# A rarely taken branch moved from between two stages to the end of the kernel

## The chip, the cores and the metric

One core of one Trainium2 chip runs the whole kernel. The metric is the device time of one execution in microseconds (us); lower is better. A core has five engines with instruction queues of their own: TensorE (PE in the profile, with its weight loads as PEld), VectorE (DVE), ScalarE (ACT), GpSimd (POOL) and SyncE (SP, which here only issues DMAs). Engines wait for one another through semaphores; a trailing q in the profile (DVEq, SPq) marks what an engine's sequencer does itself: loads of registers, branches, semaphore instructions.

## The reference, cut to what matters

Three blocks follow each other: a bucketed attention, a mixture of 8 experts in which every token goes to one expert, and a dense two-layer block.

```python
attn_out = _attn_ref(q, k, v, proj)                 # (2, 8, 768, 64)
x = attn_out.transpose(0, 2, 1, 3).reshape(1536, 512)

# experts: each token goes to the expert with the largest logit
expert_idx = np.argmax(x @ w_gate, axis=1)
for e in range(8):
    mask = expert_idx == e
    h = np.maximum(x[mask] @ w1[e], 0.0)            # 512 -> 1024
    out[mask] = gate_w[mask, None] * (h @ w2[e])    # 1024 -> 512

# last stage
h = x @ w_in                                        # 512 -> 2048
g = np.where(h > 0.0, h, np.exp(np.minimum(h, 0.0)) - 1.0)
return g @ w_out                                    # 2048 -> 512
```

## The kernel before, in words

The order of instructions on every engine is the order of the Python code (`tc.manual_schedule()`); the framework adds the semaphores, from which tile regions an instruction reads and writes.

**Attention** (`attention`) leaves the rows of x in DRAM (`g.xd`) and the gate logits in SBUF. **Routing** (`routing`) sorts the tokens by expert: `g.idx` holds for each sorted place the row it came from, `g.offi` the first place of each expert.

**Experts** (`moe`). Twelve gathers (`gather`, L762, an indirect DMA issued by POOL) fetch 128 sorted rows each. `gate` (L772, a DVE `tensor_scalar` on 128x512 fp32 in SBUF, in place) multiplies them by their gate weight, and `turn` transposes them on PE (L783) into `g.xhl`, two fp16 parts, with one ACT and one DVE instruction (L785, L789). From tile 2 on these are interleaved with the first expert's matmuls: in slot i of `rest(i)` the gates of slot i+1 are issued first, then the turns of slot i, then `more()` issues one further gather. The experts are 16 products in the order of `SEQ`; each reads a window of NW = 224 columns at an offset known only at run time. `expert_up` (L851 to L857) makes the hidden layer, `expert_down` (L869 to L876) writes columns of `g.yh` (ACT, L875) and `g.yl` (DVE, L876), one of four planes d at a time, each accumulated by 24 matmuls. Weights come in by SP (L572) into six or seven staging buffers and are split into two fp16 parts by a `Feeder` on ACT (L613) and DVE (L587 to L589, L609); during the last experts it splits `w_in` into `g.wih` and `g.wil`.

**The branch.** An expert with more than 224 tokens needs further windows. `overflow_table` lists them in `g.ovi`, with their count first. After the last expert every engine loads the count into a register (L1031) and branches on it (L1032). If it is over 0, a loop loads that expert's weights again and runs up and down for one window per round. Where a path skips such a block, each engine brings the semaphores to the values that the other path would have left.

**Last stage** (`moe2`). `stage1(b)` makes for 512 tokens 16 groups of 12 matmuls from `g.wih`, `g.wil`, `g.yh` and `g.yl` (L1087 to L1089) with an ACT, DVE and POOL chain behind each group (L1092 to L1108); `stage2` multiplies by `w_out` (L1116 to L1118) and stores by an indirect DMA from POOL that puts the rows back in order (L1122, L1123). `w_out` is loaded by SP at the start of `moe2` and split while the stage runs. PSUM is a ring of 8 banks in both stages. `body` calls `attention`, `moe` and `moe2`; L1241 is where the program ends, with drains and a barrier of all engines.

Of the kernel before, what the change touches and what calls it, by code (L numbers as in the profile page):

```python
# [9 lines left out]
F16 = mybir.dt.float16  # L10
F32 = mybir.dt.float32
I32 = mybir.dt.int32
# [3 lines left out]
PSUM = bass.MemoryType.PSUM  # L16
# [6 lines left out]
NT = B * S  # L23
DM = H * D
E = 8
# [30 lines left out]
STG = 6  # L56
# [578 lines left out]
WX = NT + NW  # L635
NOV = NT // NW
JOV = -(-NT // NW) - 1
XS, W1S, W2S, YS = 2.0 ** 6, 2.0 ** 6, 2.0 ** 7, 2.0 ** 13
# [122 lines left out]
def gather(nc, g, j, x):  # L761
    nc.gpsimd.indirect_dma_start(out=x, out_offset=None, in_=g.xd, in_offset=bass.IndirectOffsetOnAxis(ap=g.idx[:, j:j + 1], axis=0))  # L762
    g.xg[j] = x


def gate(nc, g, j, act=False):

    x, w = g.xg[j], g.gws[:, j:j + 1]
    if act:
        nc.scalar.activation(x, x, AF.Copy, scale=w)  # L770
    else:
        nc.vector.tensor_scalar(x, x, w, None, op0=ALU.mult)  # L772


def turn(tc, g, ps, js):

    nc = tc.nc
    PT = []
    for j in js:
        x = g.xg.pop(j)  # L780
        pt = ps.tile([128, 4, 128], F32, tag="mp", bufs=8, name="pt")
        for c in range(4):
            nc.tensor.transpose(pt[:, c], x[:, c * 128:(c + 1) * 128], g.id32)  # L783
        cols = slice(j * 128, (j + 1) * 128)
        nc.scalar.activation(g.xh[:, :, cols], pt, AF.Copy)  # L785
        PT.append((j, pt))
    for j, pt in PT:
        cols = slice(j * 128, (j + 1) * 128)
        nc.vector.tensor_sub(g.xl[:, :, cols], pt, g.xh[:, :, cols])  # L789


def overflow_table(tc, g, pool):

    nc = tc.nc
    sh = [1, E, JOV]
    off, n = g.oc[:, 0], g.oc[:, 1]
    jw = g.jw.unsqueeze(1).to_broadcast(sh)
    t = pool.tile([1, 4, E, JOV], F32, name="ovt")
    fl, st, pl, ex = (t[:, i] for i in range(4))
    nc.vector.tensor_tensor(fl, n.unsqueeze(2).to_broadcast(sh), jw, op=ALU.is_gt)  # L800
    nc.vector.tensor_tensor(st, off.unsqueeze(2).to_broadcast(sh), jw, op=ALU.add)
    sc = pool.tile([1, 4, 16], F32, name="osc")
    nc.vector.memset(sc, 0.0)
    en = sc[:, 3, 0:8]
    nc.vector.tensor_tensor(en, off, n, op=ALU.add)
    yield
    nc.vector.tensor_scalar(en, en, float(-NW), None, op0=ALU.add)
    nc.vector.tensor_tensor(st, st, en.unsqueeze(2).to_broadcast(sh), op=ALU.min)
    nc.vector.tensor_reduce(sc[:, 0, 8:16], fl, axis=AX.X, op=ALU.add)
    nc.vector.tensor_add(sc[:, 1, 8:16], sc[:, 0, 8:16], sc[:, 0, 7:15])  # L810
    yield
    nc.vector.tensor_add(sc[:, 2, 8:16], sc[:, 1, 8:16], sc[:, 1, 6:14])
    nc.vector.tensor_add(sc[:, 3, 8:16], sc[:, 2, 8:16], sc[:, 2, 4:12])

    nc.vector.tensor_tensor(en, sc[:, 3, 8:16], sc[:, 0, 8:16], op=ALU.subtract)
    nc.vector.tensor_tensor(pl, g.iota12[0:1, 1:1 + JOV].unsqueeze(1).to_broadcast(sh), en.unsqueeze(2).to_broadcast(sh), op=ALU.add)
    yield
    nc.vector.tensor_mul(pl, pl, fl)
    nc.vector.tensor_scalar(ex, g.iota8[0:1].unsqueeze(2).to_broadcast(sh), 8.0, None, op0=ALU.add)
    g.ovi = pool.tile([1, 1 + 2 * NOV], I32, name="ovi")  # L820
    ov = pool.tile([1, 1 + 2 * NOV], F32, name="ov")
    nc.vector.tensor_copy(ov[:, 0:1], sc[:, 3, 15:16])
    sw = [1, NOV, E * JOV]
    hw = pool.tile([1, 2, NOV, E * JOV], F32, name="hw")
    wb = g.iota12[0:1, 1:1 + NOV].unsqueeze(2).to_broadcast(sw)
    nc.vector.tensor_tensor(hw[:, 0], pl.rearrange("o e j -> o (e j)").unsqueeze(1).to_broadcast(sw), wb, op=ALU.is_equal)
    yield
    for x, o in ((ex, 1), (st, 1 + NOV)):
        nc.vector.tensor_mul(hw[:, 1], hw[:, 0], x.rearrange("o e j -> o (e j)").unsqueeze(1).to_broadcast(sw))
        nc.vector.tensor_reduce(ov[:, o:o + NOV], hw[:, 1], axis=AX.X, op=ALU.add)  # L830
    nc.vector.tensor_copy(g.ovi, ov)


def window(nc, g, pool, off):

    xw = pool.tile([128, 2, 4, NW], F16, tag="xw", bufs=2, name="xw")
    nc.vector.tensor_copy(xw[:, 0], g.xh[:, :, ds(off, NW)])
    nc.vector.tensor_copy(xw[:, 1], g.xl[:, :, ds(off, NW)])
    return xw[:, 0], xw[:, 1]


def expert_up(nc, pool, ps, wh, wl, xh, xl, step):

    hh = pool.tile([128, 8, NW], F16, tag="hh", bufs=2, name="hh")
    hl = pool.tile([128, 8, NW], F16, tag="hl", bufs=2, name="hl")
    for f in range(8):
        p = ps.tile([128, NW], F32, tag="mp", bufs=8, name="hp")
        fs = slice(f * 128, (f + 1) * 128)
        for kk in range(4):
            w = slice(kk * 1024 + f * 128, kk * 1024 + (f + 1) * 128)  # L850
            nc.tensor.matmul(p, lhsT=wh[:, w], rhs=xh[:, kk], start=(kk == 0), stop=False)  # L851
            nc.tensor.matmul(p, lhsT=wl[:, w], rhs=xh[:, kk], start=False, stop=False)
        for kk in range(4):
            w = slice(kk * 1024 + f * 128, kk * 1024 + (f + 1) * 128)
            nc.tensor.matmul(p, lhsT=wh[:, w], rhs=xl[:, kk], start=False, stop=(kk == 3))
        nc.scalar.activation(hh[:, f], p, AF.Relu)
        nc.vector.scalar_tensor_tensor(hl[:, f], p, 0.0, hh[:, f], op0=ALU.max, op1=ALU.subtract)  # L857
        step(f)
    return hh, hl


def expert_down(nc, g, ps, wh, wl, hh, hl, offs, step, pre=lambda d: None):

    s = YS / (XS * W1S * W2S)
    for d in range(4):
        p = ps.tile([128, NW], F32, tag="mp", bufs=8, name="yp")
        for kk in range(8):
            w = slice(kk * 512 + d * 128, kk * 512 + (d + 1) * 128)
            nc.tensor.matmul(p, lhsT=wh[:, w], rhs=hh[:, kk], start=(kk == 0), stop=False)  # L869
            nc.tensor.matmul(p, lhsT=wl[:, w], rhs=hh[:, kk], start=False, stop=False)  # L870
        for kk in range(8):
            w = slice(kk * 512 + d * 128, kk * 512 + (d + 1) * 128)
            nc.tensor.matmul(p, lhsT=wh[:, w], rhs=hl[:, kk], start=False, stop=(kk == 7))
        pre(d)
        nc.scalar.activation(g.yh[:, d, ds(offs[0], NW)], p, AF.Copy, scale=s)  # L875
        nc.vector.scalar_tensor_tensor(  # L876
            g.yl[:, d, ds(offs[1], NW)], p, s, g.yh[:, d, ds(offs[1], NW)], op0=ALU.mult, op1=ALU.subtract)
        step(d)


def w_items(we, x, scale, n=None):

    m = 1024 // we.shape[1]
    v = we.rearrange("(k p) f -> p k f", p=128)
    return [((v[:, c * m:(c + 1) * m], "p (k f) -> p k f", dict(k=m)), False,
             lambda c=c: tuple(a[:, 1024 * c:1024 * c + 1024] for a in x()), scale, n)
            for c in range(4)]


def moe(tc, es, g, w_gate, w1, w2, fd):  # L890
    nc = tc.nc
# [18 lines left out]
    for n in range(3, 2 * E):  # L910
        e, which = SEQ[n]
# [5 lines left out]
    for e in range(1, E):  # L917
        m = min(8, len(items) - a)
        last = e == E - 1
        n = m + XN[e] + (WO7 + 2 if last else 0)  # L920
# [10 lines left out]
    def more():  # L931
        nonlocal gathered
        if gathered < 12:

            k = gathered % 8
            gather(nc, g, gathered, g.wih.rearrange("p k f -> p (k f)")[:, k * 1024:(k + 1) * 1024].bitcast(F32))
            gathered += 1

    offs = [], []

# [87 lines left out]
    assert not fd.left()  # L1028


    n = nc.values_load(g.ovi[0:1, 0:1], min_val=0, max_val=NOV)  # L1031
    with tc.If(n > 0):  # L1032
        with tc.For_i(0, n, 1) as i:
            e = nc.values_load(g.ovi[0:1, ds(i + 1, 1)], min_val=0, max_val=E - 1)
            st = nc.values_load(g.ovi[0:1, ds(i + 1 + NOV, 1)], min_val=0, max_val=NT)
            fo = Feeder(nc, g, STG)
            fo.eager, fo.mode32 = True, ("ad", "ad")
            fo.add(w_items(w1[ds(e, 1)].rearrange("o k f -> (o k) f"), lambda: W[0], W1S))
            fo.add(w_items(w2[ds(e, 1)].rearrange("o k f -> (o k) f"), lambda: W[2], W2S))
            fo.load()  # L1040
            while fo.left():
                fo.step()
            xw = window(nc, g, pool, st)
            hh, hl = expert_up(nc, pool, ps, *W[0], *xw, lambda f: None)
            expert_down(nc, g, ps, *W[2], hh, hl, [st, st], lambda d: None)


def w_out_items(w_out, parts, cs, phase, g):
# [169 lines left out]
                moe2(tc, es3, g, w_out, out, fd)  # L1218


_INS = ["q", "k", "v", "proj", "moe_w_gate", "moe_w1", "moe_w2", "moe2_w_in", "moe2_w_out"]
_OUTS = [((NT, DM), "float32")]

# [22 lines left out]
```

## Time and profile before

| | us |
|---|---|
| three timed runs, median | 680.91 |
| lowest and highest of them | 678.58, 682.52 |
| the profiled execution, own time | 680.53 |
| its span, first to last instruction | 678.6 |

| engine | busy us | share of the span |
|---|---|---|
| PE matmul | 637.6 | 94% |
| DVE | 487.1 | 72% |
| ACT | 363.7 | 54% |
| POOL | 268.8 | 40% |

The profiled execution is inside the spread of the timed ones; 1.9 us of its time lie outside its span. The page lists 64 loads of expert weights of 512 KB each: 16 matrices in 4 pieces. With these inputs the loop of the branch thus runs no round, for a round would load 8 pieces more. Of 40 slices of the span, POOL is idle in nine in a row, from about 270 to 425 us. Attention takes the span up to about 250 us, routing and experts up to 420 us, the last stage the rest.

### The profile page before, as it was taken

What the parts mean: (1) busy time and instruction counts of PE and PEld (TensorE: products, weight loads), DVE (VectorE), ACT (ScalarE), POOL (GpSimd) and SP (SyncE); (2) the same over time, 40 slices, a digit from 0 to 9 for tenths busy, and PEclk for the clock granted to TensorE, in tenths of its full rate; (3) what the DMA queues carried; (4) which work ended last, traced back from release to release, by engine and by line L of the source; (5) the groups of instructions that cost most, each with busy time, mean ns of one, the idle gap of its engine ahead of it and who ended that gap; (6) DMA issues with size and microseconds to landing.
All of it is one profiled execution on the core that took longest, in us unless ns stands there. A gap on an engine that the chain in (4) does not pass through costs nothing. (4 is left out here: it accounts for less than half of the span.)

```text
span 678.6 us, 12321 instructions
## 1 busy us (share of the span) xinstructions
PE 637.6 (94%) x4615; PEld 422.9 (62%) x4615; DVE 487.1 (72%) x980; ACT 363.7 (54%) x664; POOL 268.8 (40%) x329
## 2 busy tenths in 40 slices
PE   5899988999999875999999998999999999999996
PEld 3456666666666644999999997444444444444442
DVE  6778989888976446899999998578788919900000
ACT  4566676667667633667666572575754237600000
POOL 4868778686854017000000000486866024411101
PEclk9989999999999998999999999999999999999999
DMA  5797999999683016477888791511111110000000
GB/s 176 159 169 174 195 268 236 203 229 197 140 142 93 13 41 204 158 272 261 292 277 307 264 286 43 202 34 55 39 37 68 52 47 16 1 15 32 23 24 31
DMA packets 124544, 92.87 MB, mean 137 GB/s; under 512 B 94273, under 2 KB 106561, under 8 KB 124481
## 3 DMA queue, kind: packets, MB, share of 16 engines
q1 hardware_dynamic: 122528, 85.76, 47.3%
q0 software_dynamic: 1952, 6.30, 2.7%
q8 instruction: 37, 0.61, 0.4%
q14 instruction: 27, 0.21, 0.1%
HBM read 62.94 MB, written 6.29 MB: 102 GB/s over the span
## 5 line engine op out<-in xcount | busy, mean ns | idle before, releaser
L1100 POOL TENSOR_SCALAR gh<-m 128x512 f16<-128x512 f32 x48 | 39.0, 812 | 198.0 <-DVE m L1099 198.0
L337 ACT ACTIVATE A<-sp,nm 128x768 f32<-128x768 f32 x96 | 95.0, 991 | 35.0 <-DVE nm L330 28.8
L319 DVE TENSOR_REDUCE nm<-sp 128x1 f32<-128x768 f32 x96 | 91.0, 948 | 25.4 <-PE sp L315 24.0
L378 ACT ACTIVATE AT<-ptA 128x512 f32<-128x512 f32 (+1 forms) x102 | 59.0, 580 | 39.5 <-PE ptA L376 32.7
L1087 PE MATMUL p<-yh,wih 128*128 128x512 f16 x192 | 73.5, 383 | 2.7 <-DVEq L1032 2.7
L388 PE MATMUL ot<-AT,vraw 128*64 128x384 f32 x192 | 74.2, 507 | 1.8 <-ACT AT L378 1.8
L1088 PE MATMUL p<-yl,wih 128*128 128x512 f16 x192 | 73.5, 383 | 0.0
L1089 PE MATMUL p<-yh,wil 128*128 128x512 f16 x192 | 73.3, 382 | 0.0
L376 PE MATMUL ptA<-id,A 128*128 128x128 f32 x396 | 61.8, 280 | 10.7 <-ACT AT L378 9.1
L314 PE MATMUL sp<-KA,QA 128*128 128x384 f16 x192 | 63.6, 331 | 3.3 <-ACT A L337 3.0
L376 PEld LDWEIGHTS ptA<-id,A 128*128 128x128 f32 x396 | 46.4, 141 | 31.4 <-ACT AT L378 26.0
L1098 DVE SCALAR_TENSOR_TENSOR m<-ex,th 128x512 f32<-128x512 f32 x48 | 37.1, 773 | 38.9 <-ACT th L1096 32.0
L315 PE MATMUL sp<-KB,QB 76*128 76x384 f16 x192 | 63.1, 329 | 0.7 <-DMA KB<-krb 0.7
L1122 ACT ACTIVATE o<-p 128x512 f32<-128x512 f32 x12 | 7.2, 597 | 86.7 <-PE p L1118 81.2
L1123 POOL DMA_INDIRECT out_dram<-o,idx x12 | 11.9, 990 | 104.8 <-ACT o L1122 102.3
L1094 ACT ACTIVATE ex<-r,lngs 128x512 f32<-128x512 f32 x48 | 34.7, 722 | 34.2 <-DVE m L1098 33.6
L347 POOL TENSOR_TENSOR hl<-A,hl 128x768 f16<-128x768 f32 x30 | 49.6, 1652 | 2.5
L1102 POOL TENSOR_TENSOR gl<-m,gh 128x512 f16<-128x512 f32 x32 | 46.2, 1444 | 2.7
L393 PE MATMUL ot<-ATD,VH 128*64 128x256 f16 x270 | 46.0, 280 | 0.0
L397 PE MATMUL ot<-AT,vraw 128*64 128x128 f32 (+1 forms) x192 | 40.0, 291 | 0.0
L358 POOL TENSOR_SCALAR hl<-A 128x768 f16<-128x768 f32 x30 | 25.0, 835 | 35.9 <-ACT A L337 35.9
L1116 PE MATMUL p<-wbh,gh 128*128 128x512 f16 x96 | 36.4, 379 | 0.1
(251 smaller groups left out, 1634.0 us busy)
## 6 DMA issues: line engine op xcount, KB each, us to landing
stg<-in_moe_w_dram SPq DMA_DIRECT2D x64, 512.0 KB, 4.6
stg<-in_moe_w_in_dram SPq DMA_DIRECT2D x16, 512.0 KB, 4.8
stg<-in_moe_w_out_dram SPq DMA_DIRECT2D x16, 512.0 KB, 3.2
vraw<-in_v_dram SPq DMA_DIRECT2D x8, 384.0 KB, 3.8
xd<-xr SPq DMA_DIRECT2D x16, 192.0 KB, 2.4
qraw<-in_q_dram SPq DMA_DIRECT2D x7, 384.0 KB, 3.9
kraw<-in_k_dram SPq DMA_DIRECT2D x7, 384.0 KB, 4.2
ATD<-hl SPq DMA_TRANSPOSE x30, 3.6
```

What stands on the lines that cost most here:

```text
L314: nc.tensor.matmul(sp[:, j, 0:384], lhsT=QA[P, h][:, c * 128:(c + 1) * 128], rhs=KA[P, h][:, kk], start=True, stop=False)
L315: nc.tensor.matmul(sp[:, j, 0:384], lhsT=QB[P, h][0:76, c * 128:(c + 1) * 128], rhs=KB[P, h][0:76, kk], start=False, stop=True)
L319: nc.vector.tensor_reduce(nm[:, 0:1], sp[:, :, 0:384], axis=AX.XY, op=ALU.max, negate=True)
L337: nc.scalar.activation(a, sp[:, :, 0:384], AF.Exp, bias=nm[:, 2:3], scale=nm[:, 1:2], accum_out=SUM[u][:, r:r + 1])
L347: LATE.append((lambda: nc.gpsimd.tensor_tensor(hl[:, 1], a, hl[:, 0], op=ALU.subtract), u, r, hl, a))
L376: nc.tensor.transpose(pt[:, cols], src[:, kt * 128:(kt + 1) * 128], g.id32)
L378: nc.scalar.activation(at[:, 0:n], pt[:, 0:n], AF.Copy)
L388: nc.tensor.matmul(ot[64:128], lhsT=vt[P][:, 1, kt, :], rhs=at, start=(kt == 0), stop=(kt == 5))
L1087: nc.tensor.matmul(p, lhsT=g.wih[:, kk, fs], rhs=g.yh[:, kk, cols], start=(kk == 0), stop=False)
L1088: nc.tensor.matmul(p, lhsT=g.wih[:, kk, fs], rhs=g.yl[:, kk, cols], start=False, stop=False)
L1089: nc.tensor.matmul(p, lhsT=g.wil[:, kk, fs], rhs=g.yh[:, kk, cols], start=False, stop=(kk == 3))
L1102: nc.gpsimd.tensor_tensor(gl[:, f], m, gh[:, f], op=ALU.subtract)
```

## The change

The branch goes from the end of `moe` to the end of `body`, behind `moe2`. Its body becomes a function `overflow`, which gathers, gates and turns all tokens once more (the windows' source was in a pool that is closed by then), and runs the loop of before; after it `moe2` runs a second time and stores every row again. Its code stands in the program twice, the second time inside the branch. `moe2` now follows the last expert directly. Since it then reads all columns of `g.yh` and `g.yl` also when some of them have not been written yet, both tiles are zeroed on POOL, right behind the twelfth gather. `g.ovi` moves to a pool that lives to the end.

```diff
-    g.ovi = pool.tile([1, 1 + 2 * NOV], I32, name="ovi")
+    g.ovi = g.cp.tile([1, 1 + 2 * NOV], I32, name="ovi")
...
@@ def more():
             gather(nc, g, gathered, g.wih.rearrange("p k f -> p (k f)")[:, k * 1024:(k + 1) * 1024].bitcast(F32))
             gathered += 1
+            if gathered == 12:
+
+                for y in (g.yh, g.yl):
+                    nc.gpsimd.memset(y.rearrange("p k t -> p (k t)").bitcast(F32), 0.0)
...
@@ end of moe()
-    n = nc.values_load(g.ovi[0:1, 0:1], min_val=0, max_val=NOV)
-    with tc.If(n > 0):
-        with tc.For_i(0, n, 1) as i:
...
+def overflow(tc, es, g, n, w1, w2):
+    nc = tc.nc
+    pool = es.enter_context(tc.tile_pool(name="ov", bufs=1, reuse_waits="tile"))
+    ps = es.enter_context(tc.tile_pool(name="ovps", bufs=1, reuse_waits="tile", space=PSUM))
+    g.xhl = pool.tile([128, 2, 4, WX], F16, name="xhl")
+    g.xh, g.xl, g.xg = g.xhl[:, 0], g.xhl[:, 1], {}
+    nc.gpsimd.memset(g.xhl[:, :, :, NT:WX], 0.0)
+    for j in range(12):
+        gather(nc, g, j, pool.tile([128, DM], F32, tag="xg", bufs=2, name="xg"))
+        gate(nc, g, j)
+        turn(tc, g, ps, (j,))
+    with tc.For_i(0, n, 1) as i:
...
@@ end of body()
                 moe2(tc, es3, g, w_out, out, fd)
+
+            n = nc.values_load(g.ovi[0:1, 0:1], min_val=0, max_val=NOV)
+            with tc.If(n > 0):
+                with ExitStack() as es4:
+                    overflow(tc, es4, g, n, w1, w2)
+                g.wo = w_out_items(w_out, (g.wb, g.wa), range(16), lambda c: 0, g)
+                with ExitStack() as es5:
+                    fd = Feeder(nc, g, STG)
+                    fd.eager = True
+                    moe2(tc, es5, g, w_out, out, fd)
```

Each zeroed tile is 128 partitions of 4 x 1760 fp16 values, written as 3520 fp32 values.

## Rows read from the trace of the kernel before

**Rows 1.** Busy us by stretch: PE, PEld, DVE, ACT, POOL; then granted clock, DMA

```profile
285.00:419.00 134.00, 133.99 (x1398) 133.73 (x1397) 132.47 (x239) 84.11 (x156) 0.00 (x0) 1.00 0.76 256
419.00:426.00 7.00, 4.35 (x17) 1.72 (x15) 3.11 (x7) 0.88 (x2) 0.00 (x0) 0.76 0.41 142
426.00:673.00 247.00, 246.84 (x1143) 111.66 (x1141) 129.88 (x176) 99.82 (x171) 95.46 (x91) 1.00 0.12 42
```

**Rows 2.** Timeline of PE around the branch: start, us, engine, line, operation [idle before]

```profile
418.66 0.93 PE L873 MATMUL yp<-hl,wah 128*128 128x224 f16 x8
422.24 0.61 PE L1087 MATMUL p<-yh,wih 128*128 128x512 f16 x1 [2.65 <-DVEq L1032]
...
425.82 0.38 PE L1087 MATMUL p<-yh,wih 128*128 128x512 f16 x1
...
428.19 0.38 PE L1089 MATMUL p<-yh,wil 128*128 128x512 f16 x1
```

**Rows 3.** Instructions of the branch line: ns min/median/max, first and last start

```profile
L1032 SPq EVENT_SEMAPHORE  x9: 17/17/17, 406.5 to 409.8; - x9
...
L1032 DVEq EVENT_SEMAPHORE  x2: 21/21/21, 422.2 to 422.3; - x2
```

**Rows 4.** The load of the count on POOL, same columns

```profile
L1031 POOLq TENSOR_LOAD <-ovi x1: 499/499/499, 380.8 to 380.8; - x1
```

**Rows 5.** Timeline of DVE before the branch

```profile
417.01 0.68 DVE L876 SCALAR_TENSOR_TENSOR yl<-yp,yh 128x224 f32 x2
...
421.14 0.39 DVE L876 SCALAR_TENSOR_TENSOR yl<-yp,yh 128x224 f32 x1
```

**Rows 6.** Timeline of ACT before the branch

```profile
414.85 0.60 ACT L875 ACTIVATE yh<-yp 128x224 f32 x2
```

**Rows 7.** Timeline of POOL: the twelfth gather

```profile
272.02 0.95 POOL L762 DMA_INDIRECT wih<-xd,idx  x1 [0.64 <-PE pt L783]
```

**Rows 8.** Groups of POOL by form: busy us, mean ns, idle before

```profile
L971 POOL MEMSET xhl<- 128x1792 f16 x1 | 1.6, 1592 | 5.7 <-PE ptA L376 5.7
```

**Rows 9.** Line 875, the writes of yh, columns as in rows 3

```profile
L875 ACT ACTIVATE yh<-yp x32: 337/357/363, 283.8 to 420.8; 128x224 f32 x32
```

**Rows 10.** Line 416, a DVE operation on 3 columns in SBUF

```profile
L416 DVE TENSOR_SCALAR rv<-sum x16: 157/1172/1523, 48.5 to 240.6; 128x3 f32<-128x3 f32 x16
```

**Rows 11.** Timeline of DVE: one instruction of line 416

```profile
48.46 1.17 DVE L416 TENSOR_SCALAR rv<-sum 128x3 f32<-128x3 f32 x1
```

**Rows 12.** Timeline of POOL at that time

```profile
47.96 1.65 POOL L347 TENSOR_TENSOR hl<-A,hl 128x768 f16<-128x768 f32 x1
```

**Rows 13.** Timeline of POOL at the start: the second of two adjoining memsets

```profile
1.78 0.61 POOL L141 MEMSET krb<- 128x624 f16 x1
```

**Rows 14.** Timeline of DVE at that time

```profile
1.31 1.16 DVE L1178 CAST id<-id 128x128 f16<-128x128 f32 x1 [1.20 <-POOL id masks.py:199]
```

**Rows 15.** Line 772, the gates

```profile
L772 DVE TENSOR_SCALAR wih<-wih,gws x11: 474/477/486, 258.9 to 283.5; 128x512 f32<-128x512 f32 x11
```

**Rows 16.** Line 1099, a DVE operation with one input in PSUM

```profile
L1099 DVE SCALAR_TENSOR_TENSOR m<-p,m x48: 690/691/694, 429.3 to 592.8; 128x512 f32<-128x512 f32 x48
```

**Rows 17.** Timeline of DVE: two gates

```profile
273.91 0.48 DVE L772 TENSOR_SCALAR wih<-wih,gws 128x512 f32<-128x512 f32 x1
...
275.22 0.48 DVE L772 TENSOR_SCALAR wih<-wih,gws 128x512 f32<-128x512 f32 x1
```

**Rows 18.** Timeline of PE: the turns that wait for these gates

```profile
276.08 0.60 PE L783 MATMUL pt<-id,wih 128*128 128x128 f32 x4
...
277.88 0.63 PE L783 MATMUL pt<-id,wih 128*128 128x128 f32 x4
```

**Rows 19.** Line 1241, the end of the program

```profile
L1241 SPq EVENT_SEMAPHORE  x13: 17/28/10237, 645.6 to 678.5; - x13
...
L1241 POOLq DRAIN  x3: 40/113/4035, 673.7 to 678.3; - x3
```

**Rows 20.** DMA queue, kind: packets, MB, share of 16 engines (page)

```profile
q8 instruction: 37, 0.61, 0.4%
```

More of the change, by code (lines that the diff above doesn't have):

```diff
@@ L1028, in moe @@
     assert not fd.left()
-    n = nc.values_load(g.ovi[0:1, 0:1], min_val=0, max_val=NOV)
-    with tc.If(n > 0):
-        with tc.For_i(0, n, 1) as i:
[L1034 to L1045, printed above, removed]
+def overflow(tc, es, g, n, w1, w2):
[10 more added lines that the diff above has]
+    with tc.For_i(0, n, 1) as i:
+        e = nc.values_load(g.ovi[0:1, ds(i + 1, 1)], min_val=0, max_val=E - 1)
+        st = nc.values_load(g.ovi[0:1, ds(i + 1 + NOV, 1)], min_val=0, max_val=NT)
+        fo = Feeder(nc, g, STG)
+        fo.eager, fo.mode32 = True, ("ad", "ad")
+        fo.add(w_items(w1[ds(e, 1)].rearrange("o k f -> (o k) f"), lambda: g.wa, W1S))
+        fo.add(w_items(w2[ds(e, 1)].rearrange("o k f -> (o k) f"), lambda: g.wb, W2S))
+        fo.load()
+        while fo.left():
+            fo.step()
+        xw = window(nc, g, pool, st)
+        hh, hl = expert_up(nc, pool, ps, *g.wa, *xw, lambda f: None)
+        expert_down(nc, g, ps, *g.wb, hh, hl, [st, st], lambda d: None)
 def w_out_items(w_out, parts, cs, phase, g):
```

## The prediction

> **What bounds the kernel now.** I first read the busy time by stretch. From 285 to 419 us PE is busy 133.99 of 134.00 us and from 426 to 673 us 246.84 of 247.00 us; only from 419 to 426 us does it drop to 4.35 of 7.00, and there the granted clock is 0.76 instead of 1.00 [rows 1]. So the second half of the kernel is one string of matmuls with one hole, the branch. What delays PE before the hole, or shortens the hole, should move the end one for one. The same rows show a second string: DVE is busy 132.47 of 134.00 us in the experts [rows 1]. A delay of DVE there cannot be made up, and what it makes last, the final `yl`, is read by the first group of the last stage.
>
> **What the move removes.** The hole, read from the timeline of PE: the last eight matmuls of the experts end at 418.66 + 0.93 = 419.59, and the next begins 2.65 us after that, at 422.24 [rows 2]. Matmuls overlap: further down one lasts 0.38 us and the next begins 0.215 us after it [rows 2], so undisturbed it would have begun 0.38 - 0.215 = 0.16 us before that end, at 419.43: 2.81 us earlier. Its releaser is a semaphore instruction of DVE on the branch line, at 422.2 [rows 2, 3]: behind a skipped block PE must have it from DVE that DVE has come past the block, and DVE comes there only when its queue is empty. Then the clock is low: 9 steps from 422.24 to 425.82 take 3.58 us, while 11 steps from 425.82 to 428.19 take 2.37, or 0.215 each [rows 2]; nine of these would be 1.94. Slow clock: 1.64 us. Removed: 2.81 + 1.64 = 4.45 us.
>
> **Does a wait take its place?** The first group of `stage1` reads the planes of `yh` and `yl` in the order 0 to 3, three matmuls each. The last plane of `yl` is written from 421.14 for 0.39, to 421.53 [rows 5]. The matmul that needs it is the eleventh, at 419.43 + 10 x 0.215 = 421.58. It comes just in time, if the framework keeps the planes apart although their columns are known only at run time. It does between ACT and DVE: ACT writes two planes of `yh` in one go from 414.85 [rows 6], before DVE has read the first of them at 417.01 [rows 5]. If PE does not stop, I take it that its clock does not fall. SP's loads of `w_out`, which stood behind the branch, can issue earlier, as staging buffers come free; the first split comes in the third group, as before, so this is worth nothing and costs nothing while the DMAs have room (busy 0.41 around the hole [rows 1]).
>
> **What the memsets add.** Two on POOL, 3520 fp32 values a partition. The nearest is 1792 values in 1.592 us [rows 8]; at the same time per value 3.13 us each. They follow the gather that begins at 272.02 and lasts 0.95 [rows 7], so about 273.0 to 276.1 and 276.1 to 279.3. ACT, which now waits for them, first writes `yh` at 283.8 [rows 9]: covered by 4 us. POOL has nothing else to do. DVE is the question. A `tensor_scalar` on three columns takes 157 ns at best and 1172 in the median [rows 10]; the one at 48.46 ends at 49.63, just behind a POOL operation that ends at 49.61 [rows 11, 12]. So some DVE operations wait until POOL's running instruction is through. One with an input in PSUM does not: 690 to 694 ns in 48 instances, whatever POOL does [rows 16]. The gates are of the first kind, SBUF to SBUF, and two of them begin under the first memset, at 273.91 and 1.31 us later [rows 17]; each has a turn on PE behind it [rows 18]. They were not lengthened by gathers (474 to 486 ns [rows 15]), but a gather is not a memset. For memsets there is one instance: a cast that began at 1.31 and lasted 1.16, to 2.47, while a memset begun 0.47 us after it ended at 2.39 [rows 13, 14].
>
> Worked out: gate A (273.91) waits for the first memset, 276.1, and ends at 276.6; its turn was due at 276.08 [rows 18], so PE is 0.5 us late. Gate B comes 0.8 us after A, at 277.4, and waits for the second memset, put back by A to 279.6, and ends at 280.1; its turn, due at 277.88 + 0.5, is 1.7 us late. PE loses 2.2 us. DVE, which catches up only while PE is stopped, ends about as late, and afterwards neither has slack [rows 1]; the whole string of experts shifts by 2.2. Bounds: 0, if memsets block no gate, to 5.3 (second rival). I take 2.2, because rows 10 to 12 show the turn changing at the end of each POOL instruction, on many more instances than the one cast.
>
> [...]
>
> **What the branch costs at the end.** Every engine loads the count and branches behind its last instruction. PE's, DVE's and SP's queues are through early and wait for the others. POOL's is last: its sequencer stands in a drain from 673.7 to 677.7 [rows 19], waiting for the last store. The load (0.5 us [rows 4]) and the jump run under that. What comes after the store is the raising of semaphores on the skipping path, POOL's own and those of its stores; nine such on SP took from 406.5 to 409.8 with waits [rows 3]. I take 0.3 us; bounds 0 (all under the drain) and 2.0 (raising behind the drain, 0.8, and a fetch of code at the jump's target: 0.4% of 16 engines' 678.6 us over 37 fetches [rows 20] is 1.2 us). Below 0 is excluded: no instruction at the end is taken away.
>
> [...] The new branch skips more code than the old one. [...]
>
> The other edits (`ovi` in another pool, code that does not run) cost nothing.
>
> **Sum.** 680.53 (the profiled execution, 0.4 below the median, inside the spread of the runs) - 4.45 + 2.2 + 0.3 = 678.6 us. I leave the 0.4 out.
>
> **Rivals.**
> 1. Memsets block no gate: -4.45 + 0.3, 676.4 us. For it: gates beside gathers [rows 15]. Against: the cast [rows 13, 14].
> 2. Slower: DVE gets no turn between the two memsets, as the cast got none before a memset that began after it. Gate A waits until 279.3 and ends at 279.7; PE is 3.65 us late at the first turn, a stop longer than the one at the branch, so the slow clock follows (1.64). 5.3 + 0.3 - 4.45 = +1.15, 681.7 us. It turns to a loss where stop and clock together pass 4.15; without the slow clock it is 680.0.
> 3. The change does not do what it says: PE still waits for all of `yl`. It then stops from 419.43 + 2.2 until 421.53 + 2.2 = 423.7, with the slow clock behind it: 1.5 us later than the 422.24 of now, and with 0.3 at the end 682.3 us. Against: rows 5 and 6.
> 4. The end costs 2.0: 680.3 us. Against: the drain covers 4 us.
>
> **How the numbers follow.** Forecast 0.42; rivals in order 0.20, 0.20, 0.07, 0.11. A measurement of this kernel tells about 0.5% from no change, 3.4 us: below 677.5 is faster, above 684.3 slower. Faster: the first rival and 0.07 of the forecast, 0.27. Slower: only two losses together, 0.05. Same: 0.68. The range from 676.0 (first rival, nothing at the end) to 681.8 (second rival) leaves out the third and sums of two rivals. Forecast and three rivals are inside; in one line, most cases are a gain at the branch that is partly paid back 140 us earlier.
>
> **What would show it.** In the trace after: no stop of PE over 0.3 us where the last stage begins, granted clock 1.00 there; POOL memsets of about 3.1 us near 273 and 276; gates of line 772 of 2 us and more beside them and PE waiting on them for 0.5 and 1.7 us. If those gates stay near 480 ns, the first rival holds; if one lasts over 5 us, the second. PE stopping for about 2 us at the stage's start would be the third. For the end: POOL's last long drain begins at 673.7 and the last instruction at 678.5 [rows 19]; these 4.8 us, counted from the load that then stands in the drain's place, should become about 5.1. The prediction is wrong if DVE makes up its delay in the experts, or if a region that I take as free delays PE at the stage's start.

## The result: 1.1% slower, above the whole range

The changed kernel takes 688.37 us (median; 687.55 to 688.93), the kernel before, run beside it, 681.04 (678.58 to 682.52): a ratio of 1.0107, interval 1.0082 to 1.0131. The forecast was 678.6, the upper end of the range 681.8. The profiled execution of after took 687.55 us, with a span of 685.65; that of before 680.53 and 678.58.

Two instructions are good marks in both traces, because what lies between them repeats to a few hundredths from run to run: the twelfth gather [rows 7] and the first matmul of the last stage [rows 2]. The third is the last store. All stretches are worked out from the starts of these instructions; "mended" is a kernel of the experiments below, changed but without the memsets and with two ACT instructions more (act2).

| stretch, us | before | after | after - before | mended |
|---|---|---|---|---|
| start to twelfth gather | 272.02 | 272.65 | +0.63 | 273.37 |
| to the first matmul of the last stage | 150.22 | 154.65 | +4.43 | 147.41 |
| to the issue of the last store | 251.68 | 251.13 | -0.55 | 250.35 |
| to the end of the span | 4.66 | 7.21 | +2.55 | 7.19 |

The first line varies between 271.5 and 276.1 over the kernels here whose code ahead of that gather is the same; 0.63 is run to run. The rest is 6.43 us, and the experiments below divide it into five terms: -2.81 (stop at the branch), -1.61 (slow clock behind it), +7.24 (memsets), +1.06 (a stop that the prediction had nowhere) and +2.55 (end of the program).

Busy time by stretch of after, columns as in [rows 1]:

```profile
270.00:286.00 16.00, 11.17 (x77) 9.81 (x76) 11.19 (x13) 4.26 (x10) 7.91 (x4) 0.73 0.35 137
286.00:427.00 141.00, 140.99 (x1469) 140.69 (x1468) 138.26 (x249) 89.18 (x164) 0.00 (x0) 1.00 0.78 260
427.00:434.00 7.00, 7.00 (x37) 3.35 (x36) 4.24 (x9) 4.00 (x8) 0.40 (x1) 1.00 0.37 126
512.00:678.00 166.00, 164.27 (x761) 74.17 (x759) 67.18 (x97) 47.73 (x81) 37.54 (x37) 1.00 0.09 31
```

Where the branch was, PE is now busy 7.00 of 7.00 us at a granted clock of 1.00, against 4.35 of 7.00 and 0.76 [rows 1]. The loss stands in the first line: between 270 and 286 us PE is busy 11.17 of 16, at 0.73.

The start of the last stage on PE, which answers to [rows 2], and the last `yl` on DVE, which answers to [rows 5]:

```profile
426.54 0.93 PE L873 MATMUL yp<-hl,wah 128*128 128x224 f16 x8
427.31 0.38 PE L1102 MATMUL p<-yh,wih 128*128 128x512 f16 x1
...
429.46 0.38 PE L1103 MATMUL p<-yl,wih 128*128 128x512 f16 x1
```

```profile
428.93 0.39 DVE L876 SCALAR_TENSOR_TENSOR yl<-yp,yh 128x224 f32 x1
```

The first matmul begins 0.16 us before the last of the experts ends, and each step is 0.215. The last plane of `yl` is there at 429.32; the eleventh matmul, which needs it, begins at 429.46.

The memsets on POOL, DVE beside them (this answers to [rows 17]), and PE:

```profile
272.65 0.94 POOL L762 DMA_INDIRECT wih<-xd,idx  x1 [1.63 <-PE pt L783]
273.59 3.05 POOL L941 MEMSET yh<- 128x3520 f32 x1
276.56 3.05 POOL L941 MEMSET yl<- 128x3520 f32 x1
```

```profile
274.54 5.35 DVE L772 TENSOR_SCALAR wih<-wih,gws 128x512 f32<-128x512 f32 x1
279.81 0.67 DVE L789 TENSOR_TENSOR xhl<-pt,xhl 128x512 f16<-128x512 f32 x1
```

```profile
274.57 0.55 PE L855 MATMUL hp<-xhl,wah 128*128 128x224 f16 x4
279.95 1.11 PE L783 MATMUL pt<-id,wih 128*128 128x128 f32 x4 [4.83 <-DVE wih L772]
```

One gate lasts 5.35 us instead of 0.48: from 274.54 to 279.89, through the rest of the first memset and all of the second, which ends at 279.61. PE stops for 4.83 us and goes on 0.06 us behind the gate. The timeline of PE in the kernel before has a row there that the prediction did not use:

```profile
274.44 0.66 PE L783 MATMUL pt<-id,wih 128*128 128x128 f32 x4
```

Counted from the twelfth gather this turn begins at 2.42 us in before and at 7.30 in after, 4.88 late; the next is 6.39 late, the one after that 7.28, and the last stage begins 7.24 late against the kernels without memsets. So 4.88 us are the wait and 2.36 the slow clock: the records of the granted clock have it at half from 278.53, late in the stop, to 285.36.

The stop of PE ahead of the second half of the last stage, and the instructions of ACT, POOL and DVE in which it starts 11 us earlier:

```profile
511.91 0.38 PE L1133 MATMUL p<-wbh,gl 128*128 128x512 f16 x1
513.51 0.38 PE L1131 MATMUL p<-wbh,gh 128*128 128x512 f16 x1 [1.21 <-DVE m L1114]
```

```profile
500.40 0.72 ACT L1109 ACTIVATE ex<-r,lngs 128x512 f32<-128x512 f32 x1 [3.63 <-DVE m L1113]
```

```profile
501.54 1.16 POOL L1117 TENSOR_TENSOR gl<-m,gh 128x512 f16<-128x512 f32 x1
```

```profile
501.74 1.50 DVE L1113 SCALAR_TENSOR_TENSOR m<-ex,th 128x512 f32<-128x512 f32 x1 [0.99 <-ACT th L1111]
```

Line 1113 reads only SBUF and takes 0.70 in the median; here it begins 0.2 us behind POOL's `gl`, waits until that ends at 502.70 and lasts 1.50, to 503.24. In the kernel before, the same `m` begins at 498.02, ahead of `gl` at 498.10, and lasts 0.69. DVE frees the banks of PSUM, so PE waits for one 1.21 us at 513.51; in before it was 0.13.

The end of the program, which answers to [rows 19]: the last store, and the sequencers' instructions on the lines of the load, the branch and the end (columns as in [rows 3]):

```profile
678.44 0.97 POOL L1138 DMA_INDIRECT out_dram<-o,idx  x1 [9.39 <-ACT o L1137]
```

```profile
L1236 POOLq TENSOR_LOAD <-ovi x1: 507/507/507, 678.2 to 678.2; - x1
...
L1237 POOLq EVENT_SEMAPHORE  x6: 17/30/43, 681.4 to 681.9; - x6
...
L1237 POOLq COMPARE_BRANCH  x1: 53/53/53, 678.8 to 678.8; - x1
L1237 POOLq INC_SWDGE_SEM  x1: 688/688/688, 682.0 to 682.0; - x1
...
L1267 POOLq DRAIN  x3: 40/107/2122, 682.7 to 685.4; - x3
```

POOL branches at 678.8 and its next instruction comes at 681.4. Six semaphores are raised by 681.9, then comes an instruction that the prediction had not seen, an increment for the semaphores of POOL's indirect DMAs (INC_SWDGE_SEM, 0.69 us), and only behind it the drain, 2.12 us from 682.7. In before the drain began 0.23 us ahead of the store's own record, at 673.7 [rows 19], and ran while the store was on its way.

### The profile page after: what moved, and what is told of

It reads as the page before. It is cut to its first block, busy times and chain, and to the rows that moved or that the text cites. A ratio compares the mean times of both kernels' runs of the same rounds, so it can differ in the third digit from the quotient of the medians.

```text
span 685.7 us, 12338 instructions
## 1 busy us (share of the span) xinstructions
PE 640.1 (93%) x4615; PEld 425.3 (62%) x4615; DVE 492.9 (72%) x980; ACT 363.5 (53%) x664; POOL 274.9 (40%) x331
## 4 chain that ended last, share of the span: by engine, by line
PE 61%; DVE 19%; ACT 11%; issue 5%; DMA 1%; POOL 1%; DVEq 0%; POOLq 0%; ACTq 0%; SPq 0%
DVE nm L319 6%; PE p L1131 5%; PE p L1132 5%; PE p L1133 5%; ACT A L337 5%; PE yp L870 4%; PE yp L873 4%; PE yp L869 4%; PE ptA L376 4%; PE hp L851 4%; PE hp L852 4%; PE hp L855 3%; PE ot L388 3%; DVE m L1113 3%; PE p L1104 2%
```

## The experiments

Theory at the start: a gate waits through the whole run of adjoining POOL instructions, and this costs some 7 us. Rivals: it is the moved stage that costs, or the end.

**Without the memsets, and the memsets alone.** Two kernels that separate the parts.

```diff
 # no_memset: the changed kernel
-                for y in (g.yh, g.yl):
-                    nc.gpsimd.memset(y.rearrange("p k t -> p (k t)").bitcast(F32), 0.0)
 # before_memset: the kernel before, branch in its old place
+                for y in (g.yh, g.yl):
+                    nc.gpsimd.memset(y.rearrange("p k t -> p (k t)").bitcast(F32), 0.0)
```

> The changed kernel without the two memsets (no other work is left out; every column that the last stage reads is written by the experts here). Theory: the memsets hold one gate for 5.35 us, PE stops 4.8 us and then runs some 6 us at half clock, about 7.3 us together; without them the kernel is at before - 4.3 (hole at the branch) + 2.6 (end of program) + 0 to 1.0 (a wait of PE for a PSUM bank in the last stage, in the changed kernel 1.2 us): 0.7 to 1.7 us below the kernel before, about 679.3 to 680.3. Rival: the loss comes from the move itself, and the time stays near 688. The PSUM wait tells two causes of it apart: if it came from DVE entering the last stage late, it goes with the memsets; if it came from where ACT's instructions now lie in the program, it stays.

> The kernel before with only the two memsets added at the same place; branch where it was. Theory: the stop of PE in the first expert and the slow clock behind it, about 7.3 us, and nothing else: 688 us. The branch's hole stays about 2.7 us of stop and 1.6 of clock. Rival of the prediction's forecast (turns change at the end of each POOL instruction): 2.2 us, 683.

Measured against the kernel before: no_memset 680.6 us, ratio 0.9964 (0.9941 to 0.9987); before_memset 688.65, 1.0083 (1.0053 to 1.0113). Line 772 of the one and of the other:

```profile
L772 DVE TENSOR_SCALAR wih<-wih,gws x11: 476/477/530, 259.2 to 285.0; 128x512 f32<-128x512 f32 x11
```

```profile
L772 DVE TENSOR_SCALAR wih<-wih,gws x11: 471/478/5355, 259.9 to 292.8; 128x512 f32<-128x512 f32 x11
```

The whole slowdown is the memsets: the same gate of 5.35 us with the branch in its old place, and none without them. From the twelfth gather to the last stage no_memset takes 147.41 us, after 154.65: 7.24. In before_memset it is 157.50 against 150.22 of before, 7.28.

Before_memset shows one thing more. Its branch makes the same stop, but the clock stays at 1.00 there (busy time from 425 to 435 us, and the first matmul of the last stage):

```profile
425.00:435.00 10.00, 7.33 (x57) 5.21 (x56) 6.16 (x13) 2.44 (x6) 0.00 (x0) 1.00 0.22 70
```

```profile
431.49 0.38 PE L1091 MATMUL p<-yh,wih 128*128 128x512 f16 x1 [2.67 <-DVEq L1036]
```

So a stop of 2.7 us has the slow clock behind it in one execution (before, 2.65 [rows 2]) and not in another; which, the trace does not show beforehand.

**How DVE gets its turn.** If the change of turn at the end of a POOL instruction is all that is needed, shorter instructions help.

```diff
 # pieces
-                    nc.gpsimd.memset(y.rearrange("p k t -> p (k t)").bitcast(F32), 0.0)
+                    z = y.rearrange("p k t -> p (k t)").bitcast(F32)
+                    for c in range(0, 3520, 440):
+                        nc.gpsimd.memset(z[:, c:c + 440], 0.0)
 # chained: as pieces, but each overlaps the one before by one column
+                        nc.gpsimd.memset(z[:, max(c - 1, 0):c + 440], 0.0)
 # by_scalar: as pieces, each a multiplication by zero
+                        nc.gpsimd.tensor_scalar(z[:, c:c + 440].rearrange("p (a b) -> p a b", b=110), src, 0.0, 1.0, op0=ALU.mult, op1=ALU.mult)
```

> The changed kernel with each memset cut into 8 of 440 values, so 16 POOL instructions of about 0.46 us back to back. If a waiting DVE instruction gets its turn at the end of a memset, a gate waits 0.5 to 0.9 us and not 5.4, and the time is the one of the kernel without memsets plus 0.5 to 2 us, 680 to 682. If memsets that stand in POOL's queue one behind the other never let DVE in, one gate waits some 6 us and the time is again 688 or more.

> As with the memsets in 16 pieces, but each overlaps the one before by a column, so that POOL waits for its own last write before the next piece. If DVE stays locked out because adjoining memsets overlap in time (each begins 0.07 us before the last ends), the gates now get their turn: 0.4 to 1 us each, PE loses under 2 us. If POOL keeps DVE out whatever stands between, one gate waits some 6 us again.

> The two tiles are zeroed in sixteen pieces of 440 values again, but each piece is a tensor_scalar that multiplies by zero instead of a memset; the pieces don't depend on one another. Theory (it is the unbroken row of POOL instructions that keeps DVE out, whatever they are): a gate of line 772 lasts over 4 us, PE stops for about as long, span about 685 to 689 us. Rival (it is peculiar to memsets; an operation that also reads leaves DVE a turn): the gates stay under 1.5 us, no stop of PE over 1 us in the first expert, span about 679 to 681 us.

Against the kernel before, pieces took 688.42 us, 1.0079 (1.005 to 1.0108); chained 681.59 in one run, beside 681.61 of before; by_scalar 691.26 in one run, beside 680.88. Lines of the zeroing and of the gates of pieces, then of chained, then of by_scalar:

```profile
L943 POOL MEMSET yh<- x8: 477/478/480, 276.1 to 278.9; 128x440 f32 x8
...
L772 DVE TENSOR_SCALAR wih<-wih,gws x11: 470/477/5910, 262.0 to 294.5; 128x512 f32<-128x512 f32 x11
```

```profile
L943 POOL MEMSET yh<- x8: 466/466/701, 275.6 to 279.6; 128x441 f32 x7, 128x440 f32 x1
...
L772 DVE TENSOR_SCALAR wih<-wih,gws x11: 471/481/762, 261.1 to 286.8; 128x512 f32<-128x512 f32 x11
```

```profile
L944 POOL TENSOR_SCALAR yh<-id x8: 547/550/573, 277.1 to 280.8; 128x440 f32<-128x440 f32 x8
L944 POOL TENSOR_SCALAR yl<-id x8: 547/547/712, 281.3 to 284.9; 128x440 f32<-128x440 f32 x8
...
L772 DVE TENSOR_SCALAR wih<-wih,gws x11: 472/480/7224, 261.8 to 295.9; 128x512 f32<-128x512 f32 x11
```

Pieces of 0.48 us do not help: the gate begins under the third of them, at 277.01, and waits through all that follow, 5.91 us. That is not peculiar to memsets; with sixteen multiplications it is 7.22 us, and there the gate gets in only ahead of the last, which lasts 0.71 us instead of 0.55. One column of overlap, by which each piece but the first of a tile waits for POOL's own last write, brings the gates to at most 0.76 us, though POOL is busy for longer: from the twelfth gather to the last stage 148.07 us, 0.66 above the kernel without zeroing. In the instructions' records these pieces of chained carry a wait for a semaphore; those of after, pieces and by_scalar carry none.

A wait on the next POOL instruction is not needed to let DVE in, though. In chained the first piece of `yl` carries none and begins 0.05 us before the piece ahead of it ends; yet a gate that began at 279.73 got in ahead of it and ended at 280.39, and the piece lasted 0.74 us instead of 0.47. In the kernel before, a DVE operation of line 173 waited for the POOL operation of line 347 that ends at 93.53, and then got in ahead of the next, which carries no wait either and lasted 0.82 us instead of 0.51. Two rows of POOL in chained, then DVE and POOL in before:

```profile
279.65 0.47 POOL L943 MEMSET yh<- 128x441 f32 x1
280.06 0.74 POOL L943 MEMSET yl<- 128x440 f32 x1
```

```profile
92.68 1.26 DVE L173 SCALAR_TENSOR_TENSOR qra<-qraw,qra 128x384 f16<-128x384 f32 x1
```

```profile
93.50 0.82 POOL L159 TENSOR_SCALAR rnd<-qraw 128x384 f32<-128x384 f32 x1
```

Of 25 DVE instructions in before that lasted over 0.4 us longer than the shortest of their line and shape, none waited on through a second POOL instruction (the cast of [rows 13, 14] is alone on its line and not among them). So adjoining POOL instructions without waits kept a gate out in after, pieces and by_scalar, but not every DVE operation everywhere. The next kernel bears on it too.

**The memsets in another place.**

```diff
 # early: out of more(), and at the start of the routing
+    for y in (g.yh, g.yl):
+        nc.gpsimd.memset(y.rearrange("p k t -> p (k t)").bitcast(F32), 0.0)
     nc.gpsimd.memset(g.xhl[:, :, :, NT:WX], 0.0)
```

> The changed kernel with the two memsets moved to the end of attention, just ahead of the memset of xhl, where POOL and DVE mostly wait for PE. If the cost lies in the place, the time is that of the kernel without memsets, 679.3 to 680.3. If they hold DVE in the short chain between attention and routing, up to 3 us more.

Measured 684.35 us, 1.0015 (0.9997 to 1.0034). Timelines of POOL, DVE and PE:

```profile
252.99 3.03 POOL L972 MEMSET yl<- 128x3520 f32 x1
255.97 1.63 POOL L973 MEMSET xhl<- 128x1792 f16 x1
```

```profile
254.67 1.39 DVE L724 TENSOR_SCALAR ai<-posi 128x12 int32<-128x12 int32 x1
```

```profile
257.70 0.19 PE L735 MATMUL ip<-rh,pm 128*128 128x12 f16 x1 [2.47 <-DVE pm L734]
```

The loss moves along: now twelve columns of the routing wait for a memset, from 254.67 to 256.06, and the routing's chain with them; the twelfth gather comes at 279.14, the latest of all kernels here. The place has no slack either. But DVE got in at 256.0, between two memsets that overlap by 0.05 us: the second of these carries waits for semaphores, met by then. So a pause is not needed; and the rows of chained and of line 173 above, with the cast of [rows 13, 14], show DVE getting in ahead of a POOL instruction that carries no wait. What exactly hands over the turn stays open.

**The end of the program.** Four more kernels without memsets: the branch goes, its body shrinks, or a hint announces it. They are compared with no_memset.

```diff
 # no_branch: without the branch and all behind it
 # short_jump: the body without its second last stage
-                g.wo = w_out_items(w_out, (g.wb, g.wa), range(16), lambda c: 0, g)
-                with ExitStack() as es5:
-                    fd = Feeder(nc, g, STG)
-                    fd.eager = True
-                    moe2(tc, es5, g, w_out, out, fd)
 # no_pool_dma: as short_jump, and in overflow()
-    nc.gpsimd.memset(g.xhl[:, :, :, NT:WX], 0.0)
-    for j in range(12):
-        gather(nc, g, j, pool.tile([128, DM], F32, tag="xg", bufs=2, name="xg"))
-        gate(nc, g, j)
-        turn(tc, g, ps, (j,))
+    nc.gpsimd.memset(g.xhl, 0.0)
 # hint: before the last tile of stage2 a hint that the branch will be taken
+                tc.mark_branch_hint_location("ov", "LikelyTaken", [mybir.EngineType.Activation, mybir.EngineType.Pool])
...
-            with tc.If(n > 0):
+            with tc.If(n > 0, label="ov"):
```

> The changed kernel without memsets and without the branch and all that it skips (left out: the work for experts with over 224 tokens, which these inputs don't need). Shows the floor. Theory: hole gone (-4.3), end of the program as in the kernel before (4.7 us from the issue of the last store to the end of the span, 7.2 to 7.5 with the branch). A wait of PE for a PSUM bank of 1.2 us as in the kernel without memsets is expected here too if it comes from where ACT's instructions lie (nothing ahead of it differs). 3.3 to 4.3 us below the kernel before.

> The changed kernel without memsets, with the second run of the last stage left out of the branch's body (never run here), so that the branch jumps less far on every engine. If the 2.66 us between branch and next instruction on ACT and POOL are a fetch of code at a far target, they fall to about 0.4 us where the target is near, and the end costs some 2 us less than without memsets alone. If they are the branch's own, they stay.

> The changed kernel without memsets, with a prefetch hint for the branch on ACT and POOL. If the stall at the jump is a fetch and the hint is heeded, 0.5 us or less in place of 2.66 between branch and next instruction; the end up to 2.2 us shorter. If not, the same as without memsets.

> Without the memsets, and the body of the branch keeps only its loop over windows: the gathers, gates and turns and the second last stage are left out of it, so it holds no indirect DMA of POOL (with these inputs the body does not run, so nothing of what is computed here changes). Theory (most of the cost at the end is the raising of the semaphores of POOL's indirect DMAs, which waits for the last store and has a drain of 2.1 us behind it): no such instruction at the end, and from the issue of the last store to the end of the span 4.7 to 5.3 us, against 6.7 with the gathers in the body and 7.5 with the stage too; time about 678.5 to 679.5 us. Rival (any skipped block with semaphores to raise costs about 2 us at the end): 6.5 us or more, and about 680.3 us.

| kernel | time, us | ratio to before | last store to end, us |
|---|---|---|---|
| no_memset | 680.6 | 0.9964 (0.9941 to 0.9987) | 7.45 |
| hint | 680.64 | 0.9992 (0.9968 to 1.0015) | 7.07 |
| short_jump | 680.23 | 0.9979 (0.9958 to 1.0001) | 6.69 |
| no_pool_dma | 680.88 | 0.9986 (0.9957 to 1.0015) | 5.14 |
| no_branch | 678.51 | 0.9965 (0.9941 to 0.9989) | 4.68 |

The branch line and the drain of short_jump, then of no_pool_dma:

```profile
L1233 POOLq EVENT_SEMAPHORE  x6: 17/30/43, 673.2 to 673.7; - x6
...
L1233 POOLq COMPARE_BRANCH  x1: 45/45/45, 672.8 to 672.8; - x1
L1233 POOLq INC_SWDGE_SEM  x1: 688/688/688, 675.4 to 675.4; - x1
```

```profile
L1258 POOLq DRAIN  x3: 40/107/2119, 676.1 to 678.8; - x3
```

```profile
L1229 POOLq EVENT_SEMAPHORE  x2: 17/17/17, 674.2 to 674.3; - x2
...
L1229 POOLq COMPARE_BRANCH  x1: 45/45/45, 674.0 to 674.0; - x1
```

```profile
L1254 POOLq DRAIN  x3: 40/107/3287, 674.7 to 678.6; - x3
```

In short_jump POOL is past the branch in 0.5 us instead of 2.7, but the increment then waits from 673.7 to 675.4. The trace records 16 landings for the last store. In short_jump the last of them comes 2.99 us behind the store's issue and the increment 0.02 later; in hint, where the jump takes 0.5 us too, it comes at 3.38 and the increment 0.02 later. So the increment waits for the store to land. In the ten kernels with the whole body and no hint it begins 0.35 to 0.67 us behind the last landing, right after the six semaphores: there the jump holds it up, and most of the far jump lies under the store's way to memory.

Without indirect DMAs in the body there is no increment; the drain begins at 674.7, ahead of the store's last landing, and ends 1.07 us behind it, as in before (1.08) and no_branch (1.07). With the increment it ends 2.87 us behind (short_jump; 2.86 in hint). Counted from the landing, the increment with the drain behind it thus costs 1.80 us, and load, branch and two semaphores nothing. But the landing itself comes later where the program ends with a branch: 2.72 to 2.73 us behind the issue in before, before_memset and no_branch, 2.84 to 3.38 in the others, because one to three of the 16 are late. Packets of instruction fetches move in that time (on queue 14 in after three of 8 KB, 0.41, 1.33 and 2.79 us behind the issue; in before none); that these delay the store is not shown. In after the 2.55 us are then 1.80 for the increment and drain, 0.33 that the jump leaves on the path, and 0.44 for the later landing (3.17 instead of 2.73); the sum is 0.02 off by rounding.

The steps of the table mix these parts: 7.45 - 6.69 = 0.76, 6.69 - 5.14 = 1.55 and 5.14 - 4.68 = 0.46, the last of which is the later landing (3.24 instead of 2.72). And kernels with the same branch and body have 7.16 to 7.47 here, so the 0.38 by which hint is shorter is hardly more than that. Three expectations were missed: short_jump was to make the end some 2 us shorter; no_branch was to lie 3.3 to 4.3 us below the kernel before, and its ratio makes it 2.4 (the medians 3.1); and the time of no_pool_dma, 678.5 to 679.5, came out at 680.88: its times run from 676.5 to 682.5, with the twelfth gather of the profiled one at 275.1. Differences of a microsecond between these kernels are read from the stretches; the medians do not carry them.

**The stop ahead of the second half of the last stage.** After, no_memset, early, short_jump and no_pool_dma have it (1.18 to 1.23 us), before, before_memset, pieces, chained, by_scalar and hint have not (0.11 to 0.18), so it goes neither with the memsets nor with the branch's place. First POOL's code and chance were tried:

```diff
 # pad: sixteen memsets of two values each in place of the two
+                    for c in range(8):
+                        nc.gpsimd.memset(z[:, 0:2], 0.0)
 # again: no_memset once more
```

> The memsets become sixteen of two values each, all of one tile on the same place, so that each waits for the one before; zeros are not written elsewhere. If the stop of PE of 1.2 us ahead of stage2 depends on where POOL's code lies, it is gone as in the kernels with sixteen pieces (0.15 to 0.18 us) and the span is about 678.4 us; if it does not, the stop stays near 1.2 us and the span is about 679.4 us.

> The same kernel as no_memset, profiled once more. If the stop of PE of 1.2 us ahead of stage2 belongs to the kernel, it is there again; if it belongs to the run, it may be 0.15 us. Span 677.5 to 680.5 us.

Both have it, 1.22 and 1.21 us: it belongs to the kernel, and POOL's number of instructions is not its cause. (Their spans, 677.4 and 681.8, miss what was expected by what comes ahead of the twelfth gather, at 271.46 and 275.80.) In these seven kernels the exponential of the 25th group (line 1109 of after, at 500.40) begins 0.34 us behind the semaphore instruction ahead of it in ACT's queue, elsewhere 0.06; it has 831 ACT instructions ahead of it in each of the seven, and 832, 833 or 838 in the six without the stop; and the next 8 KB fetch of instructions on queue 14 follows that exponential by 1.5 to 1.8 us, where in the six without the stop the last such fetch lies 4 us or more before it. That points to ACT passing from one block of code to the next just there. Two ACT instructions more, in a place where ACT is idle, would move such a passage:

```diff
 # act2: no_memset with this; after_act2: the changed kernel, memsets kept, with this
+                scr = g.cp.tile([1, 2], F32, name="scr")
+                for c in range(2):
+                    nc.scalar.activation(scr[:, c:c + 1], g.id32[0:1, 0:1], AF.Copy)
```

> Without the memsets, with two copies of one value on ACT added behind the twelfth gather, where ACT has nothing to do. Theory (in the kernels with the stop of 1.2 us ahead of stage2, ACT passes from one block of fetched code to the next exactly between the semaphore instruction and the exponential of the 25th group; one or two ACT instructions more shift the passage into a time in which ACT waits anyway): the exponential of the 25th group begins 0.06 us behind its semaphore instead of 0.34, no m lasts 1.50 us there, PE's stop ahead of stage2 is 0.15 us instead of 1.21, and the time is about 1.0 us below that of the kernel without memsets, 679.6 us, with a spread that may hide it. Rival (the stop has nothing to do with ACT's place in the code): the stop stays at 1.2 us.

> The changed kernel as it is, memsets too, with the same two ACT instructions. Theory: the stop ahead of stage2 goes to 0.15 us, everything else stays; span about 684.6 us (685.65 less 1.05), run to run within 2. Rival: the stop stays at 1.2 us.

PE of act2 at that place:

```profile
505.38 0.38 PE L1134 MATMUL p<-wbh,gl 128*128 128x512 f16 x1
505.90 0.38 PE L1132 MATMUL p<-wbh,gh 128*128 128x512 f16 x1
```

The stop is gone in both: 505.90 - 505.76 = 0.14 us, and 0.15 in after_act2, whose stretch to the last store falls from 251.13 to 250.07 us, while its gate still lasts 5.36 and the stretch ahead of the last stage is 154.74. So two ACT instructions more take the stop out of these kernels: 1.06 us. That ACT there passes from one block of code to the next is argued from the fetches and not shown.

No_branch, with one ACT instruction fewer, has a stop of 1.41 us and an exponential that is not late. Its trace has the same pattern on DVE, 33 us earlier:

```profile
474.61 1.60 DVE L1109 SCALAR_TENSOR_TENSOR m<-ex,th 128x512 f32<-128x512 f32 x1 [1.07 <-POOL gh L1111]
```

This `m` begins 0.42 us behind the semaphore instruction ahead of it in DVE's queue, against 0.07 in the median of its line, with a fetch on queue 14 at 475.27. It comes 0.10 us behind POOL's `gl`, lasts 1.60 instead of 0.70, and from there on the stage runs 1.25 us late against after_act2. No run moves DVE's code there, so this cause is argued from one trace.

In time, after_act2 took 685.96 us in one run; act2 680.49, 1.0006 (0.9985 to 1.0026), not the 679.6 expected, where the stretches alone would make it 1.6 us faster than before: 147.41 + 250.35 + 7.19 = 404.95 against 406.56.

So the version without memsets is the one to keep of the changed ones: behind the twelfth gather it is 7.0 us faster than after (406.00 against 413.00). Whether it is faster than before is open: its interval says 0.1 to 0.6%, its stretches 0.56 us (406.00 against 406.56), and short_jump, hint and act2, which do no more work in their runs, have intervals that include no change. With an expert of over 224 tokens its last stage would first read columns that nothing has written, and the second last stage would store those rows again; no run here has such inputs.

## Why the prediction was wrong, step by step

- **What bounds the kernel**: right. Nothing behind 286 us made up a delay, and DVE was busy 138.26 of 141.00 us there. What the first expert lost arrived whole at the last stage.
- **What the move removes**: right. -4.45 was forecast; the stretches give 150.22 - 147.41 = 2.81 for the stop and 251.68 - 250.07 (after_act2) = 1.61 for the clock, 4.42. Before_memset shows that the slow clock does not follow every such stop, so 1.61 of this hit hangs on the one execution that was read.
- **No wait takes its place**: right, with 0.14 us to spare in after. The third rival falls.
- **The memsets' length and place**: right; 3.05 us each against 3.13, begun 0.94 behind the gather.
- **"Rows 10 to 12 show the turn changing at the end of each POOL instruction"**: this step failed. It was read from small DVE operations beside POOL's arithmetic in attention, and carried over to a gate beside two adjoining memsets. The one instance beside memsets that I had, the cast [rows 13, 14], pointed the other way, and I set it against the number of the others. Gate A waited through both memsets, as the second rival said; the line that was to show it, a gate over 5 us, is there (5.35). Why the turn changed in the one case and not in the other stays open.
- **"Its turn was due at 276.08"**: this failed too, and it spoiled the second rival as well. The turn that waits for gate A is the one at 274.44, 0.06 us behind the gate's end in before and in after. The 1.64 us of slack that I gave it did not exist. With the right turn the second rival's own sum is 279.7 + 0.06 - 274.44 = 5.3 for the stop, and with its 1.64 for the clock 7.0: near the 7.24 measured (4.88 and 2.36).
- **The slow clock**: the forecast had none here; it lasted 6.8 us and cost 2.36, more than the 1.64 read behind the shorter stop at the branch.
- **The end**: a mis-sized term, 0.3 against 2.55, outside its bounds of 0 to 2.0. The jump was priced at 1.2 us, an estimate of one fetch of code from [rows 20]; it took 2.7 on POOL, of which 0.33 is left on the path, and 0.5 behind the hint. That the 2.7 are a fetch is not shown. What was missing is that the increment for the skipped indirect DMAs waits for the last store to land, and that the drain stands behind it instead of running beside the store (1.80 us together); the store itself also landed 0.44 later. "The load and the jump run under that" took the drain as given, though the branch stands ahead of it.
- **A region taken as free**: ACT's code moved by a few instructions, and 0.28 us there became 1.06 on PE. No row of before could have sized it; that a gap of 0.13 us at that place in before meant no reserve could have been read.

The terms are differences of stretches of the same traces, so their sum has to close, and it does: 680.53 - 2.81 - 1.61 + 7.24 + 1.06 + 2.55 = 686.96, and 0.63 of run to run ahead of the twelfth gather gives 687.59; the profiled execution took 687.55.

## What to carry to other kernels

An engine with nothing to do is not free room: its instructions can hold up another engine, and cutting them up need not help (here sixteen in a row held a gate for 5.91 and 7.22 us, two long ones for 5.35). Look for the wait that an operation has right behind it, not the one that fits the order of the code, before giving it slack. And a branch moved to the end is paid there (2.55 us in after): here what it must raise on the skipping path stood between the last store and the drain.

## What the runs showed that was not expected

- A DVE `tensor_scalar` of 0.48 us that reads and writes SBUF lasted 5.35 us beside two adjoining POOL memsets, 5.91 beside sixteen short ones and 7.22 beside sixteen multiplications, but 0.47 to 0.76 when each short one, but for the first of a tile, waited for POOL's own last write.
- The granted clock was at half for 6.8 us from late in a stop of 4.83 on, and with a stop of 2.7 us it once fell (0.76 from 419 to 426 us in before [rows 1]) and once did not (1.00 in before_memset).
- A taken branch over a large block stopped POOL for 2.7 us (after); over a smaller one (short_jump), or behind a hint (hint), 0.5.
- The increment for POOL's indirect DMAs takes 0.69 us and waits for the last store to land; a drain behind it takes 2.12 us although the last landing lies 0.7 to 1.4 us back, where one that begins ahead of the store's landing ends 1.07 or 1.08 us behind it.
- A late start of 0.28 us on ACT in the middle of a chain became 1.06 us on PE, and two ACT instructions more, 220 us earlier in the program, moved it out of the way.
